# A planner that orders a fused FFT filter and channel MLP: its landing times for some loads get an extra allowance

## The chip, the cores and the metric

The kernel runs on one core of one Trainium2 chip. The metric is the device time of one execution in microseconds (us). A core has engines that each work off their own instructions in a fixed order: PE (matrix multiplies), DVE and ACT (elementwise work; ACT also issues some transfers), POOL (elementwise work) and SP, which here does nothing but issue transfers (DMA). An instruction whose input is not there yet holds up everything behind it on its engine.

## The reference

For each of 8 batches of `x` (3136 tokens by 256 channels) the reference does this:

```python
X = np.fft.rfft(x, axis=1)
Yr = Xr @ w_r - Xi @ w_i + b_r          # complex 256x256 mix of every frequency
Yi = Xr @ w_i + Xi @ w_r + b_i
Y  = soft_threshold(Yr, 0.01) + 1j * soft_threshold(Yi, 0.01)
y  = np.fft.irfft(Y, n=3136, axis=1)
h  = y.transpose(0, 2, 1) @ U @ V       # token mix of rank 32
u  = y + h.transpose(0, 2, 1)
out = u + np.maximum(u @ w_ch1, 0) @ w_ch2   # channel MLP, 256 -> 1024 -> 256
```

## The kernel before, in words

3136 tokens are 49 x 64, so the Fourier transforms are matrix multiplies with 49-point and 64-point tables. The work on one batch has four stages, and the tile names tell them apart:

- **A**: the 49-point transform of `x`, result stored to the DRAM scratch `gd` (PSUM tile `psa`, copied by ACT to `gs`).
- **B, mix, C**: `t` is loaded from `gd`, with a table `fb`; the 64-point transform (`psb`), the complex mix (`psq`, `pst`, summed by DVE in `tb`), the threshold, a copy of half of `tb` to other partitions by DMA (`ys<-tb`), a split in two float32r parts (`yh`, `yl`), the inverse 64-point transform (`psc`) and a store to the DRAM scratch `zd` (`zs`).
- **D**: `zt` is loaded from `zd` with a table `dt`; the inverse 49-point transform (`psd`), copied to `xq`.
- **Channel MLP**: six windows of 512 tokens per batch (49 in all); `oa`, `ob`, `oc`, `od` are inputs in two parts, `psx`, `psy`, `psz` the first product, `rh`, `rl` the relu in two parts, `pso` the second product, `os` the transposed result on its way to `out`.

The MLP of batch b runs while batch b+1 is in B to D and batch b+2 in A.

For batches 3 to 7, stage A is **folded**: token row n and token row 49-n are added and subtracted first, which halves the transform. The work on a batch is 7 units (`f_load`, `f_prep`, `f_mm`). A unit needs `xt` (rows 1 to 24, straight from `x`, 240 KB), `xr` (rows 48 down to 25, 240 KB, from the DRAM scratch `xd`) and a 10 KB tail of `xr`; all three are issued by SP. `xd` is a turned copy that eight transfers issued by ACT (`f_turn`) make per batch, DRAM to DRAM. DVE then adds, `xr = xt + xr`, and later forms the difference in `xt`; ACT and POOL split each in two parts (`xh`, `xl`), and PE multiplies (`psa`). `xt` and `xr` have two buffers each.

Nothing runs in the order in which it is written. Each call is only recorded, with a cost, and `order` plans all of it: it lays the program out backward and forward twelve times, gives each unit of work a latest time, and starts on each engine whatever is ready and most urgent. What stands in the program is the resulting order on each engine; the planned times are then gone, and the semaphores alone decide when something starts. So an order that rests on a landing time that is too short shows as an engine that waits.

For a transfer, the planner takes `op.cost` 0.6 us for the issue by SP (0.35 by ACT), then `op.lag`, 2.2 us plus `op.move`, which is the number of float32 elements over 64000; `move` also advances a common clock of transfers, behind which later ones land. A load is not planned to start before its latest time less 16 us. With that the load of an `xt` of 120 x 512 elements is planned to land 0.6 + 2.2 + 0.96 = 3.76 us after its issue begins, if no other transfer is ahead of it. These are the lines:

```python
op.move = some.ids.size / 64000
op.cost = 0.35 if op.eng == "act" else 0.6
op.lag = 2.2 + op.move
...
avail[k] = max(avail[k], late[k] - units[k][0].lead)
...
moved = max(moved, t) + u.move
u.lag = moved + 2.2 - free[e]
```

`gap(e, op)` in `order` says how long after the start of `e` its successor `op` may be planned.

Of the kernel before, what the change touches and what calls it, by code (L numbers as in the profile page):

```python
# [42 lines left out]
NK, NS = 125, 120  # L43
NU = 7
TURNS = 8
FOLD = 3
X0 = (0, 80, 176)
X0_PACE = (0.98, 0.92, 0.98)
# [110 lines left out]
PASSES, LEAD, FILL = 12, 16.0, 200.0  # L159
SWITCH, STICK, MARGIN, EARLY = 0.083, 5.0, 1.0, 0.0  # L160
# [5 lines left out]


class _Op:
    __slots__ = "n eng name args kw out cost lag move port fill start preds succs unit at lead".split()


class _Program:
# [15 lines left out]
    def record(self, eng, name, args, kw):  # L188
        op = _Op()
        op.n, op.eng, op.name, op.args, op.kw = len(self.ops), eng, name, args, kw  # L190
        op.preds, op.succs, op.lead = {}, [], LEAD
        out = kw["out"] if "out" in kw else args[0]
        views = [v for v in list(args) + list(kw.values()) if isinstance(v, _View)]
        op.out = out
        self.cost(op, out, [v for v in views if v is not out])
        for v in views:
            self.access(op, v, v is out)
        if self.behind is not None and op.eng in self.only:
            op.preds[self.behind.n] = self.behind
        self.ops.append(op)  # L200
        return op
# [67 lines left out]
    def order(self):  # L269
        ops = self.ops  # L270

        units = []
        for op in ops:
            last = units[-1] if units else None
            if op.eng == "pe" and last and last[0].eng == "pe" and last[-1].n == op.n - 1:
                a, b = last[0].out.buf, op.out.buf
                if a is b or a.key[1][:3] == b.key[1][:3] == "pso" and a.space == b.space == "psum":
                    last.append(op)
                    op.unit = len(units) - 1
                    continue  # L280
            units.append([op])
            op.unit = len(units) - 1
        size = []
        for u in units:
            t = 0
            for op in u:
                op.at = t
                t += op.cost
            size.append(max(t, u[0].move) if u[0].eng == "sp" else t)
        for op in ops:  # L290
            for e in op.preds.values():
                e.succs.append(op)

        def gap(e, op):

            if e.eng == op.eng and e.name != "dma_start":
                return e.at + e.cost + CHAIN.get(e.eng, 0.0)
            return e.at + e.cost + e.lag + (MARGIN if op.eng == "pe" else 0.0)


        tags = {}
        for op in ops:
            for v in list(op.args) + list(op.kw.values()):
                if isinstance(v, _View) and v.buf.first is op and v.buf.space != "dram":
                    tags.setdefault(v.buf.key, []).append(v.buf)
                    v.buf.first = (op,)

        after = [{} for _ in units]
        for k, u in enumerate(units):
            for op in u:  # L310
                for s in op.succs:
                    if s.unit != k:
                        g = gap(op, s) - s.at
                        after[k][s.unit] = max(after[k].get(s.unit, g), g)

        ideal, t = [], 0
        for u, n in zip(units, size):
            ideal.append(t)
            if u[0].eng == "pe":
                t += n  # L320
        late = [0.0] * len(units)
        for k in reversed(range(len(units))):
            v = ideal[k] if units[k][0].eng == "pe" else ideal[k] + 30
            late[k] = min([v] + [late[j] - g for j, g in after[k].items()])
        best = None
        for _ in range(PASSES):
            end, starts, fill, reuse = self.forward(units, size, tags, gap, late)
            if best is None or end < best[0]:
                best = end, late
            late = self.backward(units, size, after, reuse, gap, starts, end)  # L330

        late = best[1]
        for seed, share, low, high in CHANGES:
            late = self.changed(late, seed, share, low, high)
        end, starts, fill, reuse = self.forward(units, size, tags, gap, late)
        for k, u in enumerate(units):
            u[0].fill = fill.get(k, 0)
            for op in u:
                op.start = starts[k] + op.at
        return end  # L340
# [207 lines left out]
def fft_mix_moe_kernel(  # L548
# [21 lines left out]
    act, dve, pool, pe, dma = [prog.engine(e) for e in ("act", "dve", "pool", "pe", "sp")]  # L570
# [83 lines left out]
    xd = [dram.tile([24, N2, D], F32, name=f"xd{k}") for k in range(2)]  # L654
# [6 lines left out]
    def rows_of(g, k0, n):  # L661
        return g[2 * k0 - 2 : 2 * (k0 + n) - 2].rearrange("(k c) n d -> (c n) k d", c=2)
# [82 lines left out]
    def f_turn(b, k):  # L745
        m = slice(N2 // TURNS * k, N2 // TURNS * (k + 1))
        v = x[b].rearrange("(n m) d -> n m d", m=N2)[48:24:-1, m]
        act.dma_start(xd[b % 2][:, m].rearrange("n m d -> m n d"), v.rearrange("n m d -> m n d"))

    def f_load(b, u):  # L750
        n0, g = (10 * u, 2) if u < NU - 1 else (N2 - 5, 1)
        v = x[b].rearrange("(n m) d -> n m d", m=N2)[:, n0 : n0 + 5 * g]
        xa = fp.tile([NK, 2, D], F32, tag="xt", name=f"xt_{b}_{u}")
        xr = qp.tile([NK, 2, D], F32, tag="zt", name=f"xr_{b}_{u}", bufs=2)
        for t, w in ((xa, v[1:25]), (xr, xd[b % 2][:, n0 : n0 + 5 * g])):
            o = t[0:NS, 0:g].rearrange("p g d -> p (g d)")
            dma.dma_start(o, w.rearrange("n (j g) d -> n j (g d)", j=5))
        dma.dma_start(xr[NS:NK, 0:g].rearrange("j g d -> j (g d)"), v[0].rearrange("(j g) d -> j (g d)", j=5))
        a_state[b, u, "f"] = (xa[:, 0:g], xr[:, 0:g], n0)

    def f_prep(b, v):
# [46 lines left out]
    def a_spread(b, lo, hi, u0=0):  # L808
        if b >= FOLD:
            return f_spread(b, lo, hi)  # L810
# [19 lines left out]
    def pairs(b):  # L830
        p = [(1 + 2 * q, 2) for q in range(12)]
        if shared(b):
            p.append((0, 2))
        elif b == 0 or b % 2 == 1:
            p.append((0, 1))
        return p
# [12 lines left out]
    def load_t(b, q):  # L849
        k0, n = pairs(b)[q]  # L850
        if b == 0:
            if (b, "fb", q) not in s_state:
                load_fb(b, q)
            ts = [[t0[h][:, k0 + k] for h in range(2)] for k in range(n)]
            s_state[b, q] = (ts, s_state.pop((b, "fb", q)))
            return
        t = fp.tile([128, 2, D], F32, tag="t", name=f"t_{b}_{q}")
        g = gd[b % 2]
        if k0:
            dma.dma_start(t, rows_of(g, k0, n))  # L860
        else:
            for k in range(n):
                dma.dma_start(t[0:64, k, :], gd[(b + k) % 2][ZERO])
        if (b, "fb", q) not in s_state:
            load_fb(b, q)
        ts = [[t[:, k, 128 * h : 128 * h + 128] for h in range(2)] for k in range(n)]
        s_state[b, q] = (ts, s_state.pop((b, "fb", q)))
# [276 lines left out]
    def z_load(b, c):  # L1144

        if b:
            tg = ("xsh", "xsl", "yh", "yl", "tb", "ys")[c % 6]
            zt = fp.tile([NP, 2, D], F32, tag=tg, name=f"zt_{b}_{c}", bufs=1)
        elif c % 8 < 2:
            zt = qp.tile([NP, 2, D], F32, tag="zt", name=f"zt_{b}_{c}", bufs=2)  # L1150
        else:
            tg, n = (("xsh", 1), ("xsl", 1), ("xh", 1), ("xl", 1), ("zs", 2), ("zs", 2))[c % 8 - 2]
            zt = fp.tile([NP, 2, D], F32, tag=tg, name=f"zt_{b}_{c}", bufs=n)
        zv = zd[b % 2].rearrange("k (j c i) d -> c (k j) i d", j=2, i=2)
        dma.dma_start(zt, zv[c])
        s_state[b, "z", c] = zt

    def u_part(v):
# [171 lines left out]
    for a in range(4):  # L1330
        v = (b_r, b_i)[a % 2]
# [607 lines left out]
    for w, prev, next_w in zip(turn_w, [None] + turn_w, turn_w[1:] + [None]):  # L1939
        b, j = divmod(w, NW)  # L1940
        if j == 0 and b < NB:
            assert not side
            side = [(6.5, lambda b=b: rest_unit(b))]
            if b + 1 < NB:
                start, mid, end = (1, 58, 84) if b else (18, 71, 86)

                side += bmc_spread(b + 1, start, mid - 6)
                if b + 2 < NB:
# [4 lines left out]
                    side += a_spread(b + 2, lo, hi, 0 if b else AHEAD_A)  # L1953
                if FOLD <= b + 3 < NB:
                    side += [(54 + 5 * k, lambda b=b, k=k: f_turn(b + 3, k)) for k in range(TURNS)]
                if b + 3 == FOLD:
                    side += [(BS - 4, f_setup)]
# [5 lines left out]
        for g in range(2):  # L1963
            l1s = l1_chunks(w, g)
            new = l2_chunks(w, g)
            for k in range(4):
                for c in range(2):
                    n = WS * j + 8 * g + 2 * k + c
# [131 lines left out]
```

## Time and profile before

| what | us |
|---|---|
| three runs | 1620.72, 1621.2, 1626.43 (median 1621.2) |
| the profiled execution, its own time | 1620.49 |
| its span in the trace | 1618.7 |
| PE busy in that span | 1582.8 (98%) |
| DVE busy | 1182.6 (73%) |
| ACT busy | 1049.1 (65%) |
| POOL busy | 533.6 (33%) |

The profile shows one execution, in us from the start of its span. The 1.8 us between span and time lie around the program. PE is close to full, so time can be taken out only where PE stands still, or where it runs at a lower granted clock. In rows of a timeline or a group, a bracket or a second column gives the idle time of the engine right before an instruction, and what ended it.

### The profile page before, as it was taken

Reading aid. Unit: us, or ns where it says so; the run is one execution under the profiler, and the core shown is the slowest. Engines: PE = TensorE matmul, PEld = TensorE weight load, DVE = VectorE, ACT = ScalarE, POOL = GpSimd, SP = SyncE. Lnnn points to the kernel's source line nnn. Section 1 sums busy time; section 2 is a strip of 40 time slices with the busy share of each in tenths; the row PEclk is TensorE's granted clock in tenths of the full one; section 3 lists DMA queues with packets and bytes.
Section 4 is the critical chain, followed back from the end, with each engine's and each line's share of the span. In section 5 each row is a group of like instructions: output and inputs, shape, how many; then the busy total and the mean of one; then the engine's idle time right before and its main releaser. Section 6 shows DMA issues by size and latency. Waiting matters only on the chain.

```text
span 1618.7 us, 31635 instructions
## 1 busy us (share of the span) xinstructions
PE 1582.8 (98%) x11034; PEld 1467.2 (91%) x11034; DVE 1182.6 (73%) x2181; ACT 1049.1 (65%) x2340; POOL 533.6 (33%) x490
## 2 busy tenths in 40 slices
PE   9999999999999999999999999999999999999998
PEld 7869999999888899999988989999988999999998
DVE  6689776677857678578856878767885677856776
ACT  4768875576665776567755778556765677655553
POOL 2213442133433443123433444213342334212221
PEclk9999999999999999999999999999999999999999
DMA  9775536237654545414674555622657234630143
GB/s 241 213 229 172 150 111 156 74 100 187 184 165 146 162 131 137 129 53 131 172 199 138 157 152 131 166 76 81 160 151 213 82 92 120 153 83 16 40 87 53
DMA packets 295141, 218.22 MB, mean 135 GB/s; under 512 B 169167, under 2 KB 251942, under 8 KB 294982
## 3 DMA queue, kind: packets, MB, share of 16 engines
q1 hardware_dynamic: 283700, 207.71, 47.6%
q10 hardware_dynamic: 11282, 8.49, 1.8%
q8 instruction: 88, 1.44, 0.4%
q14 instruction: 71, 0.58, 0.1%
HBM read 128.43 MB, written 84.09 MB: 131 GB/s over the span
## 4 chain that ended last, share of the span: by engine, by line
PE 77%; DMA 12%; DVE 3%; ACT 2%; SPq 2%; issue 2%; POOL 1%; ACTq 0%; DVEq 0%; POOLq 0%
PE pso L538 27%; PE psy L538 14%; PE psx L538 7%; PE psq L538 6%; PE psd L538 6%; PE psb L538 4%; PE psz L538 3%; PE psc L538 3%; PE pst L538 3%; DMA xt<-in_x_dram 3%; PE psa L538 3%; SPq L538 2%; DMA xd<-in_x_dram 2%; DMA ys<-tb 2%; PE psv L538 1%
## 5 line engine op out<-in xcount | busy, mean ns | idle before, releaser
L538 PE MATMUL pso<-rh,w2t 128*128 128x512 f32 (+1 forms) x1600 | 410.0, 378 | 0.0
L538 PEld LDWEIGHTS pso<-rh,w2t 128*128 128x128 f32 x1600 | 280.2, 190 | 26.4
L538 PE MATMUL pso<-rl,w2t 128*128 128x512 f32 (+1 forms) x800 | 237.8, 376 | 0.1
L538 POOL TENSOR_TENSOR yl<-ys,yh 128x512 fp32r<-128x512 f32 x98 | 127.1, 1297 | 211.4 <-ACT yh L538 92.9
L538 PEld LDWEIGHTS pso<-rl,w2t 128*128 128x128 f32 x800 | 151.5, 190 | 21.2 <-DVE rl L538 0.5
L538 ACT ACTIVATE rh<-s 128x512 fp32r<-128x512 f32 x196 | 122.5, 629 | 74.2 <-DVE s L538 73.3
L538 DVE SCALAR_TENSOR_TENSOR rl<-s,rh 128x512 fp32r<-128x512 f32 x196 | 153.5, 787 | 16.9 <-ACT rh L538 14.6
L538 POOL TENSOR_TENSOR tl<-ts,th 128x256 fp32r<-128x256 f32 x88 | 66.7, 758 | 181.0 <-ACT th L538 55.8
L538 POOL TENSOR_TENSOR ocl<-xq,och 128x256 fp32r<-128x256 f32 x47 | 36.2, 770 | 268.0 <-DVE tt L538 162.4
L538 PE MATMUL psq<-wmt,xsh 128*128 128x256 f32 (+1 forms) x704 | 122.6, 275 | 1.0 <-ACT th L538 1.0
L538 PE MATMUL psy<-odh,w1t 128*128 128x256 f32 x784 | 121.8, 278 | 0.7 <-DVE s L538 0.7
L538 PEld LDWEIGHTS psy<-odh,w1t 128*128 128x128 f32 x784 | 111.5, 192 | 6.9 <-DVE s L538 1.4
L538 PEld LDWEIGHTS psq<-wmt,xsh 128*128 128x128 f32 (+1 forms) x704 | 110.3, 191 | 4.1 <-ACT th L538 1.4
L538 PE MATMUL psd<-dt,zt 98*128 98x130 f32 x896 | 110.9, 277 | 2.6 <-DVE xq L538 1.9
L538 PEld LDWEIGHTS psd<-dt,zt 98*128 98x128 f32 x896 | 107.8, 192 | 5.0 <-DVE xq L538 2.4
L538 ACT ACTIVATE xq<-psd 128x196 f32<-128x196 f32 x256 | 70.3, 331 | 57.7 <-PE psd L538 49.9
L538 DVE TENSOR_TENSOR tb<-psq,bias 128x512 f32<-128x512 f32 x88 | 60.2, 684 | 57.8 <-DMA ys<-tb 35.1
L538 ACT ACTIVATE yh<-ys 128x512 fp32r<-128x512 f32 (+1 forms) x101 | 62.9, 623 | 60.1 <-DMA ys<-tb 49.2
L538 DVE TENSOR_TENSOR v<-v,psy 128x512 f32<-128x512 f32 x98 | 66.6, 680 | 48.2 <-ACT v L538 27.7
L538 POOL TENSOR_TENSOR xl<-xt,xh 120x512 fp32r<-120x512 f32 (+2 forms) x47 | 60.1, 1279 | 120.4 <-DVE pa L538 19.8
L538 DVE SCALAR_TENSOR_TENSOR rl<-psy,rh 128x512 fp32r<-128x512 f32 x98 | 67.0, 684 | 42.5 <-ACT rh L538 42.2
L538 PE MATMUL psq<-wmt,xsl 128*128 128x256 f32 (+1 forms) x352 | 96.8, 275 | 0.0
(234 smaller groups left out, 4255.2 us busy)
## 6 DMA issues: line engine op xcount, KB each, us to landing
zt<-zd SPq DMA_DIRECT2D x128, 196.0 KB
zd<-zs SPq DMA_DIRECT2D x96, 256.0 KB
out_dram<-os SPq DMA_DIRECT2D x188, 128.0 KB
t<-gd SPq DMA_DIRECT2D x84, 256.0 KB
fb<-in_fb_dram SPq DMA_DIRECT2D x96, 128.0 KB
vw<-vd SPq DMA_DIRECT2D x96, 128.0 KB
ys<-tb SPq DMA_DIRECT2D x175, 64.0 KB
dt<-in_fd_dram SPq DMA_DIRECT2D x112, 75.0 KB
```

The lines of the kernel that those rows point to most:

```text
L538: ins = call(*[real(a) for a in op.args], **{k: real(a) for k, a in op.kw.items()}).ins
```

## The change

Each recorded operation gets a `slack`, zero by default, that `gap` adds to the lag of an operation whose successor is on another engine (or which is itself a transfer). The three loads of a folded unit get 6.0 us, the loads `t` of stage B 2.0 us, and the loads `zt` of stage D 2.0 us from the second batch on. The eight `f_turn` transfers of a batch count twice their `move` on the planner's clock of transfers. No instruction is added or removed; only the order on the engines can differ.

```diff
+AHEAD_X = 6.0
...
-        op.preds, op.succs, op.lead = {}, [], LEAD
+        op.preds, op.succs, op.lead, op.slack = {}, [], LEAD, 0.0
...
-            return e.at + e.cost + e.lag + (MARGIN if op.eng == "pe" else 0.0)
+            return e.at + e.cost + e.lag + e.slack + (MARGIN if op.eng == "pe" else 0.0)
...
-        act.dma_start(xd[b % 2][:, m].rearrange("n m d -> m n d"), v.rearrange("n m d -> m n d"))
+        act.dma_start(xd[b % 2][:, m].rearrange("n m d -> m n d"), v.rearrange("n m d -> m n d")).move *= 2
...
-            dma.dma_start(o, w.rearrange("n (j g) d -> n j (g d)", j=5))
-        dma.dma_start(xr[NS:NK, 0:g].rearrange("j g d -> j (g d)"), v[0].rearrange("(j g) d -> j (g d)", j=5))
+            dma.dma_start(o, w.rearrange("n (j g) d -> n j (g d)", j=5)).slack = AHEAD_X
+        dma.dma_start(xr[NS:NK, 0:g].rearrange("j g d -> j (g d)"), v[0].rearrange("(j g) d -> j (g d)", j=5)).slack = AHEAD_X
...
-            dma.dma_start(t, rows_of(g, k0, n))
+            dma.dma_start(t, rows_of(g, k0, n)).slack = 2.0
...
-        dma.dma_start(zt, zv[c])
+        load = dma.dma_start(zt, zv[c])
+        if b:
+            load.slack = 2.0
```

The order differs nearly everywhere on all engines, mostly by a few places. Two places carry the argument. In names like `xt_3_3_5644`, the first two numbers are the batch and the unit (for MLP tiles the window and the half), the last is a running number that differs between the two programs.

First, DVE at the fourth folded unit of batch 3 (in the trace of before at 427 to 437 us). Before, the add `xr_3_3` stands among the first half's work of MLP window 9:

```order
L538 TENSOR_TENSOR tt_10_5679<-xq_1_16_3715,tt_10_5679 128x256
L538 TENSOR_TENSOR xr_3_3_5596<-xt_3_3_5644,xr_3_3_5596 120x512
L538 SCALAR_TENSOR_TENSOR rl_9_0_1_5700<-s5_9_0_5518,rh_9_0_1_5688 128x2x256
L538 SCALAR_TENSOR_TENSOR xt_3_3_5644<-xt_3_3_5644,xr_3_3_5596 120x512
L538 SCALAR_TENSOR_TENSOR rl_9_0_1_5700<-psy_9_0_5471,rh_9_0_1_5688 128x2x256
```

After the change the add stands behind the second half's work of the same window:

```order
L539 TENSOR_TENSOR s1_9_1_5626<-psz_9_1_5726,s1_9_1_5626 128x512
L539 TENSOR_TENSOR s5_9_1_5641<-psy_9_1_5609,s5_9_1_5641 128x512
L539 SCALAR_TENSOR_TENSOR rl_9_1_0_5721<-s1_9_1_5626,rh_9_1_0_5710 128x2x256
L539 SCALAR_TENSOR_TENSOR rl_9_1_1_5799<-s5_9_1_5641,rh_9_1_1_5762 128x2x256
L539 TENSOR_TENSOR tt_10_5697<-xq_1_16_3727 128x256
L539 SCALAR_TENSOR_TENSOR rl_9_1_1_5799<-psy_9_1_5609,rh_9_1_1_5762 128x2x256
L539 TENSOR_TENSOR tt_10_5697<-xq_1_16_3727,tt_10_5697 128x256
L539 TENSOR_TENSOR xr_3_3_5632<-xt_3_3_5702,xr_3_3_5632 120x512
L539 SCALAR_TENSOR_TENSOR xt_3_3_5702<-xt_3_3_5702,xr_3_3_5632 120x512
```

The add moved from three rows ahead of the second `rl_9_0_1` to 14 rows behind it, while on SP its load `xt_3_3` stands in both programs two rows behind the store of `gs_3_2` and ahead of the store of `zs_2_11`.

Second, SP at the fifth folded unit of batch 5 (841 to 844 us in the trace of before). Before, its loads stand behind the store of `gs_5_5`:

```order
L538 DMA vw_23_11024<-vd_805 64x512 x2
L538 DMA gd1_1054<-gs_5_5_11027 24x5x512
L538 DMA xr_5_4_11047<-xd1_5009 120x1x512
L538 DMA xr_5_4_11047<-in_x_dram 5x512
L538 DMA xt_5_4_11062<-in_x_dram 120x1x512
L538 DMA zt_4_10_11071<-zd0_478 98x512
```

After the change they stand around the store of `gs_5_4`:

```order
L539 DMA gd1_1049<-gs_5_3_10897 24x5x512
L539 DMA xr_5_4_10954<-xd1_4930 120x1x512
L539 DMA xr_5_4_10954<-in_x_dram 5x512
L539 DMA vw_23_10859<-vd_826 64x512
L539 DMA gd1_1049<-gs_5_4_10969 25x5x512
L539 DMA xt_5_4_10997<-in_x_dram 120x1x512
L539 DMA zt_4_6_11009<-zd0_480 98x512
```

The loads moved ahead of 13 rows, from `zt_4_6` to the store of `gs_5_5`; `xt_5_4` now follows directly behind the store of `gs_5_4`. The add on DVE moved a little in the other direction, from between the two `rl_22_0_0` of MLP window 22 to behind `s5_22_0`.

## Rows read from the trace of the kernel before

**Rows 1.** Windows: length, then busy time (count) by engine, clock, DMA.

```profile
0.00:130.00 130.00, 122.67 (x762) 96.33 (x763) 96.11 (x183) 83.11 (x190) 28.40 (x40) 1.00 0.81 230
...
395.00:545.00 150.00, 140.06 (x949) 129.00 (x949) 107.03 (x192) 96.38 (x219) 62.43 (x52) 0.99 0.60 168
545.00:790.00 245.00, 245.00 (x1750) 231.60 (x1750) 181.08 (x345) 166.10 (x379) 84.04 (x76) 1.00 0.47 125
790.00:990.00 200.00, 190.54 (x1307) 176.94 (x1307) 145.13 (x260) 134.23 (x306) 83.49 (x74) 0.99 0.56 159
...
1165.00:1250.00 85.00, 80.18 (x548) 73.60 (x547) 57.30 (x106) 54.06 (x121) 30.78 (x26) 1.00 0.69 191
```

**Rows 2.** Groups of instructions on DVE: busy, mean ns, idle before, releasers.

```profile
L538 DVE TENSOR_TENSOR xr<-xt,xr 120x512 f32<-120x512 f32 (+1 forms) x35 | 25.2, 721 | 47.0 <-DMA xt<-in_x_dram 27.8 <-issue 8.0 <-DMA xr<-xd 6.9
```

**Rows 3.** Timeline: a load on SP and its add on DVE, twice.

```profile
427.18 0.86 SPq L538 DMA_DIRECT2D xt<-in_x_dram  x1
...
432.21 0.69 DVE L538 TENSOR_TENSOR xr<-xt,xr 120x512 f32<-120x512 f32 x1 [1.44 <-DMA xt<-in_x_dram]
...
554.37 0.88 SPq L538 DMA_DIRECT2D xt<-in_x_dram  x1
...
566.39 0.94 DVE L538 TENSOR_TENSOR xr<-xt,xr 120x512 f32<-120x512 f32 x1
```

**Rows 4.** Chain that ended last: two of its `xt` loads, issue to landing.

```profile
880.44 5.65 DMA xt<-in_x_dram
...
936.03 4.23 DMA xt<-in_x_dram
```

**Rows 5.** Timeline of PE: first instruction after a stop, idle in brackets.

```profile
434.77 0.71 PE L538 MATMUL psz<-obh,w1t 128*128 128x256 f32 x4 [1.80 <-DVE rl L538]
...
465.87 0.83 PE L538 MATMUL psd<-dt,zt 98*128 98x130 f32 x5 [1.94 <-DVE xq L538]
...
490.29 0.34 PE L538 MATMUL psa<-xh,ffh 120*120 120x256 f32 x1 [1.35 <-DVE xq L538]
...
517.47 0.46 PE L538 MATMUL psv<-vw,pt 128*128 128x512 f32 x1 [1.28 <-ACT th L538]
...
814.62 0.60 PE L538 MATMUL psy<-obh,w1t 128*128 128x256 f32 x3 [1.71 <-DVE s L538]
...
851.99 0.48 PE L538 MATMUL psa<-xl,ffh 120*120 120x512 f32 x1 [2.42 <-POOL xl L538]
...
888.88 0.71 PE L538 MATMUL psz<-obh,w1t 128*128 128x256 f32 x4 [1.46 <-DVE rl L538]
...
959.23 0.45 PE L538 MATMUL psc<-yh,fch 128*128 128x512 f32 x1 [1.55 <-DVE tb L538]
...
1206.57 0.71 PE L538 MATMUL psy<-obh,w1t 128*128 128x256 f32 x4 [1.18 <-DVE s L538]
...
1244.10 0.48 PE L538 MATMUL psa<-xl,ffh 120*120 120x512 f32 x1 [2.67 <-POOL xl L538]
```

**Rows 6.** Windows around two stretches at half clock.

```profile
542.80:546.20 3.40, 3.40 (x12) 2.87 (x11) 3.40 (x8) 3.39 (x10) 0.40 (x1) 0.50 0.11 35
...
853.40:856.80 3.40, 3.40 (x18) 3.40 (x17) 1.36 (x3) 1.69 (x5) 0.76 (x1) 0.50 0.48 153
```

**Rows 7.** Waits of DVE and PE: us in total, times, longest.

```profile
DVE tb L538 <- DMA ys<-tb: 35.1, 27, 5.0
...
PE psa L538 <- DVE tb L538: 3.0, 2, 1.8
...
PE psd L538 <- DMA zt<-zd: 0.6, 2, 0.4
```

**Rows 8.** Waits of SP's queue: us in total, times, longest.

```profile
SPq L538 <- DMA xd<-in_x_dram: 20.8, 13, 4.9
...
SPq L538 <- POOL xl L538: 8.3, 10, 1.5
```

More of the change, by code (lines that the diff above doesn't have):

```diff
@@ L168 @@
 class _Op:
-    __slots__ = "n eng name args kw out cost lag move port fill start preds succs unit at lead".split()
+    __slots__ = "n eng name args kw out cost lag move port fill start preds succs unit at lead slack".split()
 class _Program:
```

## The prediction

> **What bounds the kernel now.** I read the windows first, because a mean over the span hides where PE stands still. PE is idle only in some stretches [rows 1]: 7.33 us in the first 130 us, then 9.94 us from 395 to 545, 9.46 us from 790 to 990 and 4.82 us from 1165 to 1250; from 545 to 790, as in the other stretches up to 1600 us, it is busy for every microsecond. The three stretches in the middle are where folded units are loaded, and together they hold 9.94 + 9.46 + 4.82 = 24.2 us. DMA share alone is not the reason: 545 to 790 has 0.47, 790 to 990 has 0.56.
>
> Next the groups, for what the engines in those stretches wait for. The add `xr = xt + xr` runs 35 times on DVE, once for each folded unit, and DVE stands idle for 47.0 us ahead of these adds, 27.8 us of it named as waits for `xt`, 6.9 us for `xr` [rows 2]. Then the timeline, for how late the loads are. The load issued at 427.18 lets its add go at 432.21, 5.03 us later, and DVE waited 1.44 us for it; the one issued at 554.37 has its add at 566.39, 12.02 us later, and there is no wait [rows 3]. In the chain that ended last, `xt` loads take from 4.23 to 5.65 us [rows 4]. The planner counts 3.76 us where nothing is ahead of the load, so wherever it puts the add as early as its plan allows, the add comes 0.5 to 1.9 us too early, plus whatever SP is late.
>
> Last, PE's own stops. DVE is in order, so the waiting add holds up `rl`, `s`, `tb` and `xq` rows that PE needs next. Ten stops of PE follow such a wait, 1.80 + 1.94 + 1.35 + 1.28 + 1.71 + 2.42 + 1.46 + 1.55 + 1.18 + 2.67 = 17.36 us [rows 5]; I put a stop here if an `xr` add that had waited ends within 3.6 us before it. The releaser named is the row behind the add (`rl`, `xq`, `s`, `tb`), or a later step of the same work (`xl`). So 47.0 us of waits cost PE 17.36 us, 0.37 us for each us. What is left of the 24.2 us is 6.86 us: waits around `ys<-tb`, for which DVE stands idle 35.1 us in the whole span and behind which PE stops for 3.0 us on `tb`, and small ones [rows 7].
>
> Two stretches of 3.4 us at 0.50, that is 1.2 instead of 2.4 GHz, are in the same place [rows 6]. The second begins 1.4 us after PE's stop of 2.42 us at the add of 848 us. At half speed 3.4 us of work cost 1.7 us more.
>
> **The change, part by part.** No instruction is added, so there is no cost of that kind; PE, DVE and ACT have the same work.
>
> *The three loads of a unit, 6.0 us.* The planner now keeps at least 3.76 + 6.0 = 9.76 us between issue and add, against a measured 5.65 us at most: 4.1 us to spare, which also covers an SP that is late. The order shows that it is kept, in two ways. At unit 3 of batch 3 the load stays where it was and the add moves by 17 rows on DVE; with 192 rows in 150 us [rows 1], 0.78 us a row, that is 13 us, and the wait of 1.44 us there [rows 3] needs only 1.44. At unit 4 of batch 5 the loads move ahead of 13 rows on SP, and the add stays about where it was. The engines that were waiting then find the data there: gain between 0 (the waits only change their name) and 17.36 us. I take all of it, because the pair of 12.02 us shows what such a distance does. The stop of 2.42 us goes with it, and so should the half clock behind it: 1.7 us.
>
> Moving the add costs nothing by itself while PE has other work, which it has: `xl`, `psa` and the store of `gs` come later by as much, and the next user of `gs` is stage B of the next batch.
>
> *`t` and `zt`, 2.0 us.* Between 0 and the 0.6 us in which PE waits for `zt` [rows 7]; I take 0.6 us. No stop of PE is put down to `t`.
>
> *`f_turn` counted twice.* It moves `xr<-xd` later behind its eight transfers. SP waits for `xd` 20.8 us in 13 waits [rows 8], with everything behind it late. What this costs PE is in the ten stops already (those at 517 and 959 us follow adds that waited for `xr<-xd`), so no second gain is counted.
>
> *What comes late next.* A load that is wanted 6 us earlier is issued as soon as its buffer is free: there are two each of `xt` and `xr`, and POOL's `xl` is their last reader. SP then waits for POOL, and `ys<-tb`, `out` and `zd` stand behind it. Before, SP waits for `xl` ten times, 8.3 us in all, 1.5 us at most [rows 8]. If it becomes 70 waits (both loads of 35 units) of up to 1.5 us, that is 0 to 105 us of SP, and at DVE's rate of 0.37 between 0 and 39 us of PE. The nearest row is the mean of the ten, 0.83 us; but only part of the loads will find POOL late, as ten did before. I take the remaining 6.86 us of stops as growing by half, 3.4 us, which at 0.37 stands for 9 us more of waits on SP.
>
> *The first 130 us* are reordered too, by single places. The bounds are the 7.33 us of idle PE there as a gain, and one more stop like the largest of the ten, 2.67 us, as a loss; I take 0.
>
> The sum against the profiled execution: 1620.5 - 17.4 - 1.7 - 0.6 + 3.4 = 1604.2. That execution lies 0.7 us below the median of the three runs, 1621.2, which is within their spread; I say **1604 us**, 1.1% under the median. A difference of less than 0.5%, about 8 us, is about what a measurement of this kernel can't tell from no change.
>
> **The rivals.**
>
> *All of it goes.* If the stops for `ys<-tb` end too, because SP is no longer late, then 24.2 us and both half-clock stretches (3.4 us) go: 1620.5 - 27.6 = 1593. For it: the stretch from 545 to 790 has the same `ys` transfers and no stop. Against: `ys<-tb` gets no allowance. Chance 0.08.
>
> *SP becomes the wait.* SP held 0.5 us by each of the 70 loads is 35 us, at 0.37 13 us given back: 1620.5 - 19.7 + 13 = 1614. For it: in the second place of the order `xt_5_4` stands directly behind a store, at the buffer's release, with the `zt` loads behind it. Against: the loads don't have to be exact any more, and `ys` rows stand behind only some of them. Chance 0.18, of which half is under 1613, the bound of 0.5%.
>
> *Slower.* The same with the full 1.5 us at each of the 70: 105 us of SP, 39 us of PE, 1620.5 - 19.7 + 39 = 1640. It becomes slower than before where the mean hold is over 19.7 / 0.37 / 70 = 0.76 us. The mean of the ten is above that, but ten of 70 are not all. Chance 0.05.
>
> *Nothing happens.* If it is not the landing of the loads that ends the waits, a longer planned landing buys nothing: 1620. Against it: the add of [rows 3] goes 0.1 us after its load's 4.9 us are over, and 5.65 us stand in the chain as one transfer [rows 4]. For it: 8.0 us of the 47.0 are named "issue" [rows 2]. Chance 0.05. The Trainium skill speaks for this rival (DMA: Bandwidth & Descriptors, Anatomy of one DMA): it fits 2.0 us plus the bytes over 436e3 to one transfer, on GpSimd's path, which for 245,760 bytes makes an estimate of 2.6 us, less than the planner counts already. The trace disagrees, with 4.23 to 5.65 us on SP's path, beside other transfers, and the measurement decides.
>
> **How the numbers follow.** Forecast 0.64, with 1597 to 1611 as its own range (the give-back between 0 and 6.86 us, and the first 130 us). With the rivals: faster by over 0.5% (under 1613) 0.64 + 0.08 + 0.09 = 0.81; within 0.5% 0.09 + 0.05 = 0.14; slower by over 0.5% 0.05. The range of 1595 to 1615 leaves out most of the first rival, a third of the second, the slower case and the case of nothing, about 2 in 10.
>
> **What would show it.** Right: idle of DVE ahead of the 35 adds falls from 47.0 to under 10 us; PE idle in the three folded stretches falls from 24.2 to about 10 us; no half clock after 850 us. Wrong: `xr` adds that still wait; or SP waits on `xl` rising from 8.3 to over 40 us, with DVE's waits for `ys<-tb` well over 35.1 us and new stops of PE behind `tb` and `yl`; or new stops in stretches that had none, which would mean that the new order as a whole is worse.

## The result, and the profile after

The changed kernel took 1604.92 us (median of 4 runs, 1603.29 to 1609.4), the kernel before on the same chip 1621.32 us (4 runs, 1620.72 to 1626.43). The ratio is 0.9896, with a 95% interval of 0.9867 to 0.9926: 16.4 us less, against 1604 forecast. The profiled execution, the fastest of the four, took 1603.29 us. From the page, its span, its engines and the chain's shares (the chain of before is 77% PE and 12% DMA):

```profile
span 1601.5 us, 31600 instructions
...
PE 86%; DMA 6%; DVE 4%; ACT 2%; SPq 2%; issue 1%; POOL 0%; ACTq 0%; DVEq 0%; POOLq 0%
```

The windows of after, to be held against [rows 1] and [rows 6] (columns as there: stretch, its length, busy time of PE, PEld, DVE, ACT and POOL, granted clock, DMA share, GB/s):

```profile
0.00:130.00 130.00, 124.04 (x783) 99.64 (x784) 101.73 (x191) 87.93 (x199) 28.02 (x41) 1.00 0.83 238
...
395.00:545.00 150.00, 146.50 (x996) 135.83 (x996) 111.79 (x195) 98.10 (x220) 60.52 (x53) 0.99 0.59 168
545.00:790.00 245.00, 242.45 (x1741) 228.87 (x1740) 188.57 (x350) 168.92 (x383) 84.28 (x77) 1.00 0.48 130
790.00:990.00 200.00, 197.67 (x1381) 185.59 (x1381) 152.82 (x274) 141.95 (x320) 86.82 (x76) 1.00 0.59 166
...
1165.00:1250.00 85.00, 81.11 (x554) 74.84 (x553) 61.24 (x108) 56.12 (x126) 36.39 (x30) 1.00 0.60 165
...
sum 1601.50, PE 1577.70 PEld 1466.71 DVE 1193.68 ACT 1055.11 POOL 530.67; mean PE 175.30 PEld 162.97 DVE 132.63 ACT 117.23 POOL 58.96
...
429.90:433.30 3.40, 3.40 (x9) 2.62 (x9) 1.95 (x4) 1.94 (x4) 1.29 (x2) 0.50 0.51 115
```

PE is now idle for 3.50, 2.33 and 3.89 us in the three folded stretches, 9.7 us against 24.2. The stretch from 545 to 790, which had no idle time, has 2.55 us, and another such stretch, from 990 to 1165, has a stop of 0.92 us (at 1025.82, below). Over the span PE's idle time is 1601.5 - 1577.7 = 23.8 us, against 1618.7 - 1582.8 = 35.9. One stretch of 3.4 us at half clock is left of two, at another place. So the 17.2 us by which the span fell are 12.1 us less idle and 5.1 us less "busy" for the same 11034 matmuls. Of the latter 1.7 us are the half clock.

Next the group of the adds, against [rows 2], and the waits, against [rows 7] and [rows 8] (total us, times, longest):

```profile
L539 DVE TENSOR_TENSOR xr<-xt,xr 120x512 f32<-120x512 f32 (+1 forms) x35 | 25.9, 739 | 2.5 <-DMA dt<-dud 2.5
```

```profile
DVE tb L539 <- DMA ys<-tb: 28.6, 22, 3.1
...
PE psd L539 <- DMA dt<-dud: 3.9, 3, 2.4
PE psv L539 <- ACT gs L539: 2.3, 1, 2.3
...
PE psa L539 <- DVE tb L539: 1.8, 1, 1.8
...
SPq L539 <- POOL xl L539: 20.6, 20, 3.5
...
SPq L539 <- DMA xd<-in_x_dram: 9.1, 9, 3.3
```

The adds wait for 2.5 us in place of 47.0, and for no load of `x` at all. SP waits for POOL's `xl` 20 times and 20.6 us, where it had been ten times and 8.3 us; the wait for `xd` fell from 20.8 to 9.1 us. PE now waits for `dt<-dud`, a load of a part of the table `dt` of stage D; before, its list of waits had no such row. The timeline shows PE's four largest stops and one of the smaller ones (start, us, what, and in brackets the idle time ahead of it), and the chain the transfers ahead of three of them:

```profile
428.97 0.48 PE L539 MATMUL psv<-vw,pt 128*128 128x512 f32 x1 [2.31 <-ACT gs L539]
429.29 0.38 PE L539 MATMUL psc<-yh,fch 128*128 128x512 f32 x1
429.51 0.38 PE L539 MATMUL psc<-yh,fcl 128*128 128x512 f32 x1
...
560.26 0.48 PE L539 MATMUL psa<-xh,ffh 125*125 125x512 f32 x1 [1.80 <-DVE tb L539]
...
834.20 2.03 PE L539 MATMUL psd<-dt,zt 98*128 98x130 f32 x16 [1.24 <-DMA dt<-dud]
...
1025.82 1.16 PE L539 MATMUL psd<-dt,zt 98*128 98x130 f32 x8 [0.92 <-DVE pa L539]
...
1230.02 2.04 PE L539 MATMUL psd<-dt,zt 98*128 98x130 f32 x16 [2.40 <-DMA dt<-dud]
...
427.29 0.63 ACT L539 ACTIVATE yh<-ys 128x512 fp32r<-128x512 f32 x1 [3.47 <-DMA ys<-tb]
```

```profile
423.08 4.44 DMA zd<-zs
...
554.27 5.03 DMA ys<-tb
...
1224.26 5.67 DMA dt<-dud
```

The stop at 428.97 stands behind ACT, which had been held for 3.47 us by a `ys<-tb` copy. The chain goes by way of a store of `zs`, but that landed at 427.52 (423.08 + 4.44), when ACT had been at work again since 427.29. The stop at 560 follows a `tb` behind such a copy, and those at 834 and 1230 wait for `dt<-dud`. None of these transfers has an allowance in the planner.

**PE's stops, counted by the prediction's rule.** The prediction put a stop of PE behind an add if an `xr` add that had waited (here over 0.05 us) ended within 3.6 us before PE's first instruction after the stop. The table applies this to every idle time of PE of 0.5 us or more after the first 130 us, summed over the timeline of each profiled execution (worked out from all of its rows; the kernels are explained below, under Experiments).

| kernel | adds wait, us | PE stops behind such adds, us | other PE stops, us | both | span, us |
|---|---|---|---|---|---|
| before | 47.0 | 17.4 | 4.8 | 22.1 | 1618.7 |
| before, shaken 1 / 2 | 44.1 / 51.6 | 19.8 / 24.3 | 8.8 / 4.6 | 28.6 / 28.9 | 1630.5 / 1628.9 |
| `t`, `zt` alone | 50.2 | 16.9 | 1.2 | 18.1 | 1617.0 |
| `f_turn` alone | 39.7 | 13.8 | 7.8 | 21.6 | 1617.0 |
| the change with 0 us for `x` | 31.0 | 5.4 | 3.2 | 8.6 | 1606.9 |
| the change with 2.0 us | 24.8 | 3.2 | 4.9 | 8.1 | 1599.0 |
| the same, shaken 1 | 17.0 | 0 | 6.0 | 6.0 | 1594.4 |
| **the change (6.0 us)** | 2.5 | 0 | 11.5 | 11.5 | 1601.5 |
| the same, shaken 1 / 2 | 0.3 / 1.9 | 0 / 0 | 11.7 / 8.5 | 11.7 / 8.5 | 1599.1 / 1599.4 |
| the change with 14.0 us | 0.1 | 0 | 13.2 | 13.2 | 1604.3 |
| 6.0 us for `x` alone | 0.0 | 0 | 14.7 | 14.7 | 1609.2 |

By this count the change took away all 17.4 us of stops behind waiting adds and got 6.8 us of other stops in their place (4.8 to 11.5). Two things limit the table. It counts what is near, so it can't tell a stop that an add caused from one that only came after it. And each row is a single execution, while executions of one kernel differ by several us: those of runs 1 to 4 below are the slowest of their kernels (for run 1, 1611.42 us where the fastest took 1601.76), that of the changed kernel is the fastest of its four. So differences of a few us between rows may be this scatter.

Half clock follows some of the stops, and the columns of stops do not count it. In the first shaken order of the kernel before, four stretches at 0.50 sum to 17.0 us, in the second to 13.6 us, against 6.8 us in [rows 6]; the longest is this one, with the first instruction after the stop that it goes with:

```profile
868.92 1.45 PE L538 MATMUL psd<-dt,zt 98*128 98x130 f32 x5 [5.03 <-DVE xq L538]
```

```profile
868.60:875.40 6.80, 6.48 (x25) 6.11 (x26) 4.13 (x9) 4.58 (x11) 3.46 (x4) 0.50 0.28 76
```

The execution of run 1 has 10.2 us at 0.50.

### The profile page after: what moved, and what is told of

The parts are those of the page before. It is cut to its first block, busy times and chain, and to the rows that moved or that the text cites. A ratio compares the mean times of both kernels' runs of the same rounds, so it can differ in the third digit from the quotient of the medians.

```text
span 1601.5 us, 31600 instructions
## 1 busy us (share of the span) xinstructions
PE 1577.7 (99%) x11034; PEld 1466.7 (92%) x11034; DVE 1193.7 (75%) x2181; ACT 1055.1 (66%) x2340; POOL 530.7 (33%) x490
## 4 chain that ended last, share of the span: by engine, by line
PE 86%; DMA 6%; DVE 4%; ACT 2%; SPq 2%; issue 1%; POOL 0%; ACTq 0%; DVEq 0%; POOLq 0%
PE pso L539 28%; PE psy L539 16%; PE psx L539 7%; PE psd L539 7%; PE psq L539 6%; PE psb L539 5%; PE psz L539 4%; PE psc L539 4%; PE psa L539 3%; PE pst L539 3%; DMA ys<-tb 2%; SPq L539 2%; PE psv L539 1%; DMA dt<-dud 1%; DVE tb L539 1%
## 5 line engine op out<-in xcount | busy, mean ns | idle before, releaser
L539 DVE SCALAR_TENSOR_TENSOR rl<-s,rh 128x512 fp32r<-128x512 f32 x196 | 159.7, 819 | 26.2 <-ACT rh L539 23.2
L539 PEld LDWEIGHTS pso<-rl,w2t 128*128 128x128 f32 x800 | 151.6, 189 | 20.8
L539 DVE TENSOR_TENSOR v<-v,psy 128x512 f32<-128x512 f32 x98 | 66.6, 680 | 43.1 <-ACT v L539 28.9
L539 DVE TENSOR_TENSOR tb<-psq,bias 128x512 f32<-128x512 f32 x88 | 60.2, 684 | 47.6 <-DMA ys<-tb 28.6
L539 PE MATMUL psb<-fb,t 128*128 128x128 f32 (+1 forms) x700 | 93.3, 276 | 0.9 <-DVE tb L539 0.6
```

The costliest lines, as they stand in the source:

```text
L539: ins = call(*[real(a) for a in op.args], **{k: real(a) for k, a in op.kw.items()}).ins
```

## The experiments

After the result these theories stood. **Theory 1**: the allowance on the folded loads ends the waits of the adds, and that is the gain. **Theory 2**: the gain comes from the other edits, `f_turn` counted twice or the 2.0 us on `t` and `zt`. **Theory 3**: the kernel before is an unlucky order, and nearly any other order would do as well. After the first four runs two more were formed: **theory 4**, each part helps and an order adds a random part of some 0.4%; **theory 5**, the parts overlap, because they take away the same stops and leave others.

All kernels compute the whole result. They ran in three groups of four, each group with its own runs of before, whose medians were 1625.26, 1623.51 and 1626.11 us, so the ratios are what is to be compared.

**1. Only the 6.0 us for `x`.**

```diff
-...rearrange("n m d -> m n d")).move *= 2
+...rearrange("n m d -> m n d"))
-            dma.dma_start(t, rows_of(g, k0, n)).slack = 2.0
+            dma.dma_start(t, rows_of(g, k0, n))
-            load.slack = 2.0
+            load.slack = 0.0
```

> One part alone: only the three loads of a folded unit get 6.0 us; t, zt and f_turn are as before. Theory 1 (the allowance on the folded loads ends the waits of DVE ahead of the adds, and the stops of PE behind them): idle ahead of the 35 adds under 8 us (47.0 before, 2.5 after), time 1602 to 1609, so at least three quarters of the 16.4 us. Theory 2 (the gain comes from t, zt and f_turn): 1616 to 1622. Theory 3 (any other order would do, the time is a draw): anywhere from 1603 to 1622, with no tie to the idle time ahead of the adds.

Measured: 1608.7 us (6 runs, 1601.76 to 1611.42), ratio 0.9891 [0.9871, 0.9912]. The adds wait for nothing, and yet PE stops elsewhere (in the profiled execution, the slowest of the six); first the group of the adds, then two rows of the timeline:

```profile
L539 DVE TENSOR_TENSOR xr<-xt,xr 120x512 f32<-120x512 f32 (+1 forms) x35 | 24.9, 711 | 0.0
```

```profile
935.25 0.45 PE L539 MATMUL psa<-xh,ffh 120*120 120x512 f32 x1 [2.50 <-DVE tb L539]
1223.20 2.07 PE L539 MATMUL psd<-dt,zt 98*128 98x130 f32 x8 [3.31 <-DMA dt<-dud]
```

The allowance alone gives 1.1%, as much as the whole change. Theory 1 holds as far as that.

**2. The change without it.**

```diff
-AHEAD_X = 6.0
+AHEAD_X = 0.0
```

> The other part alone: the allowance of the folded loads is 0.0; t, zt (2.0 us) and f_turn (counted twice) as in the change. Theory 1: the adds still wait, 30 to 50 us in all, and the time is 1614 to 1622. Theory 2: 1603 to 1609 with few waits. Theory 3: anywhere between.

Measured: 1605.25 us (4 runs, 1603.56 to 1608.7), ratio 0.988 [0.9863, 0.9897].

```profile
L539 DVE TENSOR_TENSOR xr<-xt,xr 120x512 f32<-120x512 f32 (+1 forms) x35 | 27.5, 787 | 31.0 <-DMA xt<-in_x_dram 18.5 <-issue 3.2 <-DMA dt<-in_fd_dram 2.5
```

The other two edits give as much without the 6.0 us. The time is in the range of theory 2 and 9 us under that of theory 1, though the "few waits" that theory 2 expected did not come. The adds still wait for 31.0 us, but the stops of PE behind them are 5.4 us in place of 17.4. That is against theory 1 as the only cause, and against any fixed price for a wait.

**3 and 4. 2.0 and 14.0 us in place of 6.0.**

```diff
-AHEAD_X = 6.0
+AHEAD_X = 2.0
```

and the same with 14.0.

> The change with 2.0 us instead of 6.0 us for the folded loads: planned 5.76 us from issue to landing, against 4.23 to 5.65 us in the chain of before, so about enough for the transfer and nothing for a late SP. Theory 1: idle ahead of the adds between the two, 5 to 20 us, time 1605 to 1613. Theory 2: as the change, 1603 to 1609, whatever the adds wait. Theory 3: no order among 0, 2, 6 and 14 us.

> The change with 14.0 us for the folded loads. There are two buffers each, and POOL reads them last, so loads can't go out as early as the plan would like; either they stand on SP right at the release of a buffer (SP waits on xl well over the 20.6 us after the change), or the units themselves are put later. Theory 1: no waits ahead of the adds (under 4 us), but nothing more to gain over 6 us, and what SP and the later stages lose shows: 1603 to 1615. Theory 3: a draw, anywhere from 1600 to 1622.

Measured: with 2.0 us 1598.08 us (4 runs, 1594.25 to 1600.78), ratio 0.9831 [0.9813, 0.985]; with 14.0 us 1604.4 us (4 runs, 1601.75 to 1606.08), ratio 0.9866 [0.9848, 0.9885]. With 2.0 us the adds wait for ten times as long as in the changed kernel:

```profile
L539 DVE TENSOR_TENSOR xr<-xt,xr 120x512 f32<-120x512 f32 (+1 forms) x35 | 27.5, 785 | 24.8 <-DMA xt<-in_x_dram 14.8 <-issue 6.9 <-DMA xd<-in_x_dram 3.1
```

With 14.0 us nothing is left of that wait, and PE stops for others, as two rows of its timeline show:

```profile
446.92 1.34 PE L539 MATMUL psd<-dt,zt 98*128 98x130 f32 x6 [2.77 <-DMA dt<-dud]
524.94 0.45 PE L539 MATMUL psv<-vw,pt 128*128 128x512 f32 x1 [2.56 <-DVE tb L539]
```

Less of the add's wait is not less time: the smallest allowance of the three is the fastest kernel, and its 1598 us lie under what theories 1 and 2 expected. It has stops for a load as well, there for `zt`, and a load of `x` can take longer than the 3.76 + 2.0 us that its plan keeps at least; a row of its waits and one of its chain:

```profile
PE psd L539 <- DMA zt<-zd: 4.4, 4, 2.7
```

```profile
862.38 8.10 DMA xt<-in_x_dram
```

**5 and 6. The kernel before, shaken.** Before the last forward pass a normally distributed number of 0.1 us is added to each unit's latest time. That gives another order of the same planner with the same landing times; the first number is the seed.

```diff
-CHANGES = ()
+CHANGES = ((1, 0.1, 0.0, 1e9),)
```

and the same with seed 2.

> The kernel before, with the planner's latest times shaken by normal noise of 0.1 us, which changes the order in some 340 of 2183 places on DVE and no landing time. After the first four runs the kernel without the 6.0 us is as fast as the change, so theory 1 is in doubt. Theory 1 (the short landing times cost the time): still 35 to 55 us of waits ahead of the adds, and a ratio of 0.996 to 1.004 to the kernel before. Theory 3 (the order before is an unlucky draw, and nearly any other order is faster): ratio 0.986 to 0.993, although the adds wait as long.

> The same with another seed of the noise. Theory 1: ratio 0.996 to 1.004 again. Theory 3: 0.986 to 0.993, or a spread between this and the other seed of more than 0.5%.

Measured: 1627.69 us (12 runs, 1618.53 to 1635.76), ratio 1.003 [1.0009, 1.005], and 1631.15 us (12 runs, 1623.37 to 1640.55), ratio 1.0047 [1.0026, 1.0069]. The groups of the adds, of seed 1 and of seed 2:

```profile
L538 DVE TENSOR_TENSOR xr<-xt,xr 120x512 f32<-120x512 f32 (+1 forms) x35 | 26.4, 755 | 44.1 <-DMA xt<-in_x_dram 18.2 <-DMA zt<-zd 7.1 <-issue 6.8
```

```profile
L538 DVE TENSOR_TENSOR xr<-xt,xr 120x512 f32<-120x512 f32 (+1 forms) x35 | 25.8, 736 | 51.6 <-DMA xt<-in_x_dram 30.6 <-DMA xr<-xd 7.2 <-issue 6.6
```

With the old landing times any of the three orders waits for 44 to 52 us ahead of the adds, and both new ones are a little slower (the second lies just above the 0.996 to 1.004 of theory 1). Theory 3 falls, as far as two orders close to the old one can show it.

**7. `f_turn` counted twice, alone**, and **8. the 2.0 us on `t` and `zt`, alone.**

```diff
-AHEAD_X = 6.0
+AHEAD_X = 0.0
-            dma.dma_start(t, rows_of(g, k0, n)).slack = 2.0
+            dma.dma_start(t, rows_of(g, k0, n))
-            load.slack = 2.0
+            load.slack = 0.0
```

is the first; the second has `AHEAD_X = 0.0` and `f_turn` without `.move *= 2`.

> One part alone: only the f_turn transfers count twice; no allowance for any load. Theory 1: 0.996 to 1.004, with 35 us or more of waits ahead of the adds. Theory 2a (the gain of the run without the 6.0 us came from f_turn, because SP no longer waits for xd): ratio 0.986 to 0.991, SP's wait for xd well under the 20.8 us before. Theory 3: anywhere from 0.985 to 1.002.

> One part alone: only t and zt get their 2.0 us. Theory 1: 0.995 to 1.002. Theory 2b (the gain of the run without the 6.0 us came from t and zt): 0.986 to 0.991. Theory 3: anywhere from 0.985 to 1.002.

Measured: `f_turn` alone 1613.02 us (11 runs, 1610.78 to 1619.88), ratio 0.9942 [0.9924, 0.996]; `t` and `zt` alone 1621.09 us (12 runs, 1615.78 to 1627.86), ratio 0.9984 [0.9967, 1.0001]. The groups of the adds, of the first and of the second:

```profile
L539 DVE TENSOR_TENSOR xr<-xt,xr 120x512 f32<-120x512 f32 (+1 forms) x35 | 25.8, 736 | 39.7 <-DMA xt<-in_x_dram 27.2 <-DMA dt<-in_fd_dram 3.7 <-DMA gd<-gs 3.1
```

```profile
L539 DVE TENSOR_TENSOR xr<-xt,xr 120x512 f32<-120x512 f32 (+1 forms) x35 | 24.4, 697 | 50.2 <-DMA xt<-in_x_dram 39.0 <-DMA xr<-xd 3.8 <-DMA dt<-in_fd_dram 3.8
```

`f_turn` by itself gives 0.6%, between the ranges of theory 1 (0.996 to 1.004) and theory 2 (0.986 to 0.991); 0.2% for `t` and `zt` is not told from nothing. So run 8 serves as a control: an allowance on loads for which PE hardly waited leaves the adds' waits (50.2 us) and the time about where they were. The parts alone give 1.09 + 0.58 + 0.16 = 1.8%, and all three together 1.0%; the last two together give 1.2% (run 2), where they add up to 0.7. So, as single orders, they don't add.

**9 and 10. The changed kernel, shaken** with seeds 1 and 2, and **11. the kernel with 2.0 us, shaken** with seed 1; the line is that of runs 5 and 6, in run 11 beside `AHEAD_X = 2.0`.

> The change, with the planner's latest times shaken by normal noise of 0.1 us (seed 1), as was done with the kernel before, where it moved the ratio to 1.003 and 1.005. Theory 4 (each part helps, x by about 1.1%, f_turn by 0.6%, t and zt by 0.2%, and each order is besides a draw of some 0.4%, so that 6.0 us drew badly): ratio 0.977 to 0.990, the mean of the two seeds below the 0.9896 of the change. Theory 5 (the parts overlap, and what is left after any two of them is other waits): 0.987 to 0.993 for both seeds.

> The same with seed 2. Theory 4: 0.977 to 0.990. Theory 5: 0.987 to 0.993. The spread between the two seeds says how much of any difference between single orders is the draw.

> The change with 2.0 us for the folded loads (0.983 in the earlier run, the best so far), shaken with seed 1. If 2.0 us is really better than 6.0 us: 0.980 to 0.986. If that run was a good draw: 0.986 to 0.992, as the change. Idle ahead of the adds again 15 to 35 us in either case.

Measured: 1603.08 us (6 runs, 1600.87 to 1604.19), ratio 0.9859 [0.9835, 0.9883]; 1598.6 us (6 runs, 1594.68 to 1603.45), ratio 0.9834 [0.9806, 0.9861]; with 2.0 us 1596.7 us (6 runs, 1593.97 to 1601.23), ratio 0.9829 [0.9801, 0.9858]. The group of the adds in the last, where the waits of 17.0 us have no stop of 0.5 us or more behind them:

```profile
L539 DVE TENSOR_TENSOR xr<-xt,xr 120x512 f32<-120x512 f32 (+1 forms) x35 | 25.5, 729 | 17.0 <-DMA xt<-in_x_dram 9.9 <-DMA xd<-in_x_dram 3.2 <-DMA dt<-dud 2.5
```

The three orders with 6.0 us have ratios of 0.9896, 0.9859 and 0.9834, the two with 2.0 us 0.9831 and 0.9829. Each ratio is known to about 0.3%. All five lie under all three of the old landing times (1, 1.003, 1.0047) by at least 1%, which is the change; among themselves they differ by up to 0.7%, most of it between orders with the same 6.0 us. Both shaken orders with 6.0 us lie in the range of theory 4 (0.977 to 0.990, their mean under 0.9896) and below that of theory 5 (0.987 to 0.993). That 2.0 us is better than 6.0 is suggested by the means (0.983 and 0.986), but one order with 6.0 is as fast, so it is not settled.

**12. An allowance for the wait that is left:** 4.0 us on the three loads of `dt`, for which PE waits 3.9 us in the changed kernel.

```diff
+AHEAD_DT = 4.0
...
-                dma.dma_start(two(dt_)[:, :, e, c], two(c_fd[:, TI * t : TI * t + TI, :])[:, :, e, c])
-            dma.dma_start(u_part(dt_), u_store(t))
+                dma.dma_start(two(dt_)[:, :, e, c], two(c_fd[:, TI * t : TI * t + TI, :])[:, :, e, c]).slack = AHEAD_DT
+            dma.dma_start(u_part(dt_), u_store(t)).slack = AHEAD_DT
```

> The change, and the three table loads dt of stage D (two from the input, one from the scratch dud) get an allowance of 4.0 us. After the change the longest stops of PE in the folded stretches but one end with dt from dud (3.9 us in 3 waits, 2.4 the longest). If those are late landings that cost time: the waits of psd for dt under 1 us, and 2 to 5 us less than the change, ratio 0.986 to 0.988. If other waits take their place or the draw decides: 0.987 to 0.993.

Measured: 1603.85 us (6 runs, 1598.07 to 1608.1), ratio 0.9866 [0.9839, 0.9893]. That is in the range expected if the late landings of `dt` cost time (0.986 to 0.988), but also within what the three orders of the changed kernel give (0.9834 to 0.9896), so it is no sign of a gain. The waits of PE for DVE's `pa` in it, and the larger of them in the timeline:

```profile
PE psd L540 <- DVE pa L540: 6.3, 2, 4.4
```

```profile
835.62 1.68 PE L540 MATMUL psd<-dt,zt 98*128 98x130 f32 x8 [4.43 <-DVE pa L540]
```

PE's stops for `dt<-dud` are down to one of 0.59 us, but the same `psd` at 835 us now waits 4.43 us for DVE. All its stops sum to 13.0 us, against 11.5: in this execution the wait was replaced, not removed.

## Why the prediction came out right, and where it was not

**The mechanism: right.** The adds waited for loads that the planner lets land too early, and with 6.0 us more they don't: 47.0 to 2.5 us, forecast under 10. All ten stops of [rows 5] are gone; no stop behind a waiting add is left in any order with 6.0 us or more. Runs 5 and 6 show that it is not the shuffling of the order that did it. One step on the way does not follow from the rows it names: the DMA share is 0.56 to 0.69 in the stretches with stops and 0.47 in the one without [rows 1], so the stops do go with it. That the share is not the reason is shown by the change: 0.59 to 0.60 in the same three stretches, with 9.7 us of idle time in place of 24.2.

**The give-back: mis-sized, and by another way.** The step "I take the remaining 6.86 us of stops as growing by half, 3.4 us" is the term that was too small. By the same count the other stops grew by 6.8 us, twice as much, and PE's idle time fell by 12.1 us. Half of the growth lies where the prediction looked for it: in the three folded stretches the other stops went from 4.8 to 8.2 us, and the idle time there fell to 9.7 us, "about 10" as forecast. The other 3.3 us are stops in the stretches from 545 to 790 and from 990 to 1165, which had none and for which the sum had no term. The forecast way was SP held by `xl`. SP's wait for `xl` did grow, by 12.3 us against "9 us more", but its wait for `xd` fell by 11.7 us, and DVE's waits for `ys<-tb`, which stand behind SP, fell from 35.1 to 28.6 us. And over the runs SP's wait for `xl` does not go with the stops: run 1 has 8.5 us of it and the most other stops, 14.7 us, while the first shaken order of the changed kernel has 12.6 us of it and 11.7 us. What does go with a large allowance is a wait of PE for `dt<-dud`: 3.9 us in the changed kernel, 3.3 in run 1, 4.9 in run 4, 1.2 and 3.9 in runs 9 and 10; with 0 or 2.0 us it is 0.8 us at most, though run 3 has 4.4 us of waits for `zt<-zd` instead. Why it comes was not tried; run 12, where it is all but gone, is no faster than the orders of the changed kernel are.

**"0.37 us for each us": not a rate.** With the old landing times, the 44 to 52 us of waits cost PE 0.37 to 0.47 for each us (17.4 / 47.0, 19.8 / 44.1, 24.3 / 51.6). In run 2 it is 5.4 / 31.0 = 0.17, in run 3 3.2 / 24.8 = 0.13, in run 11 nothing for 17.0 us. This fits a wait of DVE costing PE something only where PE has run out of other work by then, which was not tried by itself; the first part of the waits that went took most of the stops along. So the last 17 to 25 us of waits, which the 6.0 us removes and the 2.0 us does not, had about 3 us of stops behind them at most, and the other stops in the orders with 6.0 us are 2.5 to 6.8 us more than in those with 2.0 us (8.5 to 11.7 against 4.9 to 6.0).

**"No second gain is counted" for `f_turn`: not borne out as a statement on the edit.** Alone it gives 0.6%, where the prediction had nothing. In one sense it was right: it acts on the same stops, 17.4 to 13.8 us behind the adds in its one profile, and on top of it and of `t` and `zt` the 6.0 us gives between -0.2% and 0.5% (0.988 against 0.9896, 0.9859 and 0.9834). So the gain of the change is not the 6.0 us alone, as the sum had it: either half of the change takes out about 1.1 or 1.2%. The count of stops speaks for theory 5, that the parts overlap: run 1 leaves none of the 17.4 us and run 2 leaves 5.4, so 12.0 us of them go by either half. An overlap is also what the planner's lines would give, since a doubled `move` puts off the planned landing of every transfer behind it, loads of `x` included; that this is the reason was not tried. But the shaken orders lie outside theory 5's range and in theory 4's, and run 2 is more than its two parts by some 0.5%, as much as orders differ among themselves. So theory 4's random part is in every one of these ratios; which of the two theories holds, and how much each part is worth to better than about half a per cent, stays open.

**Half clock and "busy": right in sum.** One of two stretches went, 1.7 us as forecast, and none came after 850 us; but a new one stands at 430 us, behind a new stop, and both of [rows 6] are gone. The other 3.4 us of "busy" that vanished were no term of the prediction. Where matmuls follow each other they start 0.22 us apart and are drawn 0.38 us long (`psc` around 429.5 us), so at each stop up to 0.16 us of standing still may be drawn as work; over the seven stops fewer (20 of 0.5 us or more in the whole span before, 13 after) that would make some 1.1 us, and the rest was not resolved.

**Why the sum hit: in part by luck.** Terms put on record: 17.4 + 1.7 + 0.6 - 3.4 = 16.3 us. Measured in the span: 17.2 us. Stops behind adds 17.4 and the half clock 1.7 came out as said; `zt` gave 0.1, not 0.6 (PE still waits 0.5 us for it); the give-back was 6.8 in place of 3.4 and holds that too; and two things that the sum had at nothing made up for it, 1.4 us less idle time in the first 130 us and the 3.4 us of "busy": 17.4 - 6.8 + 1.7 + 1.4 + 3.4 = 17.1. Also, the changed kernel is the slowest of its three orders: with another seed the same reasons would have met 0.9834, some 10 us lower, which is the case "all of it goes" in time, without being that case (8.5 us of other stops are still there).

**The other rivals.** "SP becomes the wait" and "slower" had their condition in part (20.6 us of waits on `xl`, not the 40 named), without the `tb` waits that should follow. The last sign of being wrong, stops in stretches that had none, came in small (2.55 and 0.92 us), without the new order being worse as a whole. "Nothing happens" is excluded by run 1.

## What to carry to other kernels

When a planner's landing time is shorter than the trace's, the engines that wait show it, and a small correction takes out most of what it costs: here 2.0 us did as much as 6.0 or more. Don't price an engine's waits at one rate; count the stops of the engine that bounds the kernel, sorted by what is ahead of them, before and after, for a wait that is removed can show up again as another, and remember that a profile is one execution. And where a change re-plans everything, run two or three shaken orders of either side before a difference under about half a per cent is given to a cause.

## What the runs showed of the hardware that was not expected

A stop of about the same length is followed by half clock in one place and not in another: in the changed kernel 2.31 us at 428.97 is followed by 3.4 us at 0.50, and 2.40 us at 1230.02 is not (that stretch has a granted clock of 1.00). A small transfer can take as long to land as a large one, beside other traffic: of the loads that were waited for, a `dt<-dud` of 49 KB takes 5.67 us in the chain of the changed kernel, where `xt` loads of 240 KB took 4.23 to 5.65 us in that of before [rows 4]. Its size, from the list of transfers:

```profile
dt<-dud SPq DMA_DIRECT2D x56, 49.0 KB
```
